# FAVOR attention and a float64 bilinear FFN on one core: whole projections, fillers in early gaps, the clamp on GpSimd, pairs from chunk 6

## The chip, the core and the metric

The kernel runs on one core of a Trainium2 chip. The metric is device microseconds of one execution; lower is better. The times shown are medians over a few runs, and one further execution was taken with the hardware profiler.

The engines are TensorE (PE in the rows; PEld is its weight load), VectorE (DVE), ScalarE (ACT), GpSimd (POOL) and SyncE (SP, which issues most of the DMAs). Each works through its own list of instructions in order.

## The reference: what is computed

Eight sequences of 576 tokens, eight heads of 64 channels, go through an attention with random features; its output, 4608 tokens of 512 channels, goes through a bilinear feed-forward part whose four weights come as float64.

```python
def phi(x):                       # x scaled by 64 ** -0.25
    proj = einsum('bhsd,md->bhsm', x, omega)          # 128 features
    h = proj - sum(x * x, -1, keepdims=True) / 2
    return exp(h - max(h, -1, keepdims=True)) / sqrt(m)
q_p, k_p = phi(q_s), phi(k_s)
kv  = einsum('bhsm,bhsd->bhmd', k_p, v)
num = einsum('bhsm,bhmd->bhsd', q_p, kv)
den = einsum('bhsm,bhm->bhs', q_p, sum(k_p, 2))[..., None] + 1e-06
x = (num / den) -> [4608, 512]
a = x @ w1                        # float64 weights, 512 x 1024
b = x @ w2
out = ((a * b) @ w3) @ w_out      # 1024 x 1024, 1024 x 512
```

The kernel folds `w3 @ w_out` into one matrix `W` of 1024 x 512 on the chip.

## The kernel before

**Tiling.** Tokens go in 36 chunks of 128. For a chunk of k or of q, `features` (line 681) projects eight heads onto 128 features. Operands have 64 rows (one head), so two matmuls, one on the upper and one on the lower 64 rows of the array, stand side by side. Chunks that come early (`whole`) are projected in fp32, 8 matmuls; the later ones (55 projections) are split into two fp16 halves and take three passes, 24 matmuls `pa<-om,hl`. Then VectorE reduces (`s_nm<-pa`) and subtracts, ScalarE takes the exponential, and the result is split into fp16 halves `ek` or `eq`. `kv_batch` sums k features times v, `q_attend` (826) multiplies q features with that, `x_turn` splits and transposes the result into `xT`.

**The feed-forward part.** For chunks below `SG` = 8, `gate` (1127) multiplies `xT` with both weights; from chunk 4 on it takes two chunks at a time, 192 matmuls of 256 columns for two chunks. From chunk `SG` on, `pair_turn` (877) and `pair_gate` (1244) work on two chunks with seven products where eight are usual: 2 x 7 x 24 = 336 matmuls of 128 columns for two chunks, with weight sums that `mix` (1171) makes beforehand on GpSimd. `project_out` (1284) multiplies with `W`: 24 matmuls of 512 columns for a chunk.

**The float64 weights.** `from_float64` (966) turns a piece of 128 x 1024 doubles into fp32: DMA, absolute value on ScalarE, then on VectorE a clamp (`TENSOR_SCALAR arena<-arena` f32), a shift and mask (the same name, uint32) and two combinations (`SCALAR_TENSOR_TENSOR` into `arena`, then into `w12b`). There are 20 such pieces, one of them cut in two; three raw buffers hold them. `W_block` (1065) multiplies w3 with w_out in fp32, 8 products of 8 matmuls `pm<-w12b`.

**What sets the order.** All operations are first recorded, in an order given by a table of slots; consecutive matmuls into the same PSUM tile are joined to one operation of at most `JOIN` = 8 parts (record, line 219). Then a planner (`order`, 411) gives every operation a cost (`cost`, 279), runs a list schedule forwards (`forward`, 322), once backwards for ranks, forwards again, and emits every engine's instructions in the order of the planned starts. Operations cannot be interleaved within: an operation of 8 matmuls is the unit that may alternate with other work. PSUM has two tags: `pa`, two tiles of two banks for projections, kv and attention, and `pm`, four banks for everything else. Nearly all rows carry line 168, the helper that fires a recorded operation, so rows are told apart by their tiles.

Of the kernel before, what the change touches and what calls it, by code (L numbers as in the profile page):

```python
# [8 lines left out]
F32 = mybir.dt.float32  # L9
# [5 lines left out]
ALU = mybir.AluOpType  # L15
# [40 lines left out]
SPARE = 'oh'  # L56
KQ = 's'
TAIL = 2
SG = 8
MIX_N = 3  # L60
MIX_E = 'p'
SUM_E = 'p'
# [139 lines left out]
    return name, p, p + ap.partition_size(), lo * w, hi * w  # L202


def flat(a):
    return a.ap if isinstance(a, View) else a


class Plan:
# [9 lines left out]
    def record(self, lane, method, args, kwargs):  # L219
# [59 lines left out]
    def cost(self, op):  # L279

        out = op.out
        n = out.free_size()
        m = max([n] + [a.free_size() for a in op.ins])
        if op.lane == "tensor":
            t = 0
            for p in op.parts:
                c = p.out.free_size() / 2.4 + 2.5
                if p.ins[0].dtype == F32:
                    c = 4 * p.out.free_size() / 2.4 + 5
                if p.ins[0].partition_size() == 64:  # L290
                    c = c / 2 + 2
                t += max(c, 27)
            return t, t + 170
        if op.method == "dma_start":
            size = n * out.partition_size() * mybir.dt.size(out.dtype)
            return {"sync": 330, "scalar": 100, "gpsimd": 680}[op.lane], size / 330
        if op.method == "dma_start_transpose":
            return 2140, 1300
        thin = [a for a in op.ins if a.free_size() == 1 and m > 1]
        if op.lane == "vector":  # L300
            wide = [a for a in op.ins if a.free_size() > 1]
            if op.method == "memset":
                t = 10 + 0.8 * n * mybir.dt.size(out.dtype) / 4
            elif op.method == "reciprocal":
                t = 85 + 4 * n
            elif op.method == "tensor_reduce" or len(wide) > 1:
                t = 72 + 1.1 * m + (60 if thin else 0)
            else:
                t = 68 + 0.53 * m + 45 * len(thin)
            return t, t + 85  # L310
        if op.lane == "scalar":
            t = (130 if thin else 60) + 0.9 * m + (60 if "accum_out" in op.kwargs else 0)
            return t, t + 95
        if op.method == "memset":
            t = 40 + 0.85 * n
        elif op.method == "tensor_tensor":
            t = 95 + 2.0 * m
        else:
            t = 100 + 1.0 * m
        return t, t + 50  # L320

    def forward(self, rank, deps, after, costs, slots=False):
# [4 lines left out]
        dma = 0.0  # L327
        free, todo, slot, line = {}, {}, {}, {}
        if slots:
            for g in self.gens:  # L330
# [23 lines left out]
        for _ in self.ops:  # L354
# [15 lines left out]
            busy, lat = costs[op]  # L370
# [40 lines left out]
    def order(self):  # L411
# [12 lines left out]
        best = None  # L424
        self.seen = []
        plain = {o: set(o.deps) for o in ops}
        for n in range(ROUNDS):
            start, total, slot = self.forward(rank, plain, turned(plain), costs, True)
            self.seen.append(total)
            deps = self.chained(start, slot)  # L430
            after = turned(deps)
            for m in range(INNER + 1):
                if m:
                    start, total, _ = self.forward(rank, deps, after, costs)
# [4 lines left out]
                late, _, _ = self.forward(  # L439
                    back, {o: set(after[o]) for o in ops}, {o: list(deps[o]) for o in ops}, costs  # L440
                )
                rank = {o: -late[o] - costs[o][0] for o in ops}
        _, start, slot = best
        for g, k in slot.items():
            g.slot = k
        return sorted(ops, key=lambda o: (start[o], o.index))

    def emit(self):
        before = {}
# [3 lines left out]

ROOM = {"xhl1": 1024}
BANKS = ("pm", "pa")
JOIN = 8
HOP = 60
ROUNDS = 1
INNER = 2
AHEAD = 500  # L460
# [3 lines left out]
def tile_favor_attention_then_bilinear_ffn(  # L464
# [41 lines left out]
    ps = Slots(nc, ps)  # L506

    def banks(name):
        return ps.tile([P, 2, 512], F32, tag="pa", name=name, bufs=2)
# [6 lines left out]

    ones_bf = const.tile([P, P], BF16, name="ones_bf")
    nc.vector.memset(ones_bf, 1.0)
    ln_e = const.tile([P, 1], F32, name="ln_e")
    nc.vector.memset(ln_e, 15 * math.log(2.0))  # L520

# [6 lines left out]
    def pick(kinds, i):  # L528
        return kinds[min(i, len(kinds) - 1)]
# [426 lines left out]
    left = {}  # L956
    converted = []
    nfetch = [-1]

    def used(at):  # L960

# [4 lines left out]
    def from_float64(new, src, name, cuts=1):  # L966
# [551 lines left out]
```

## Time and profile before

| | before |
|---|---|
| median of 3 runs | 839.0 us (838.31 to 839.31) |
| the profiled execution | 838.5 us, of which span 836.7 us |
| PE busy | 773.0 us, 92% |
| DVE busy | 627.6 us, 75% |
| ACT busy | 476.2 us, 57% |
| POOL busy | 376.5 us, 45% |

Shares over the whole span hide that the program has stages: float64 conversion and the first chunks (to about 200 us), attention and gates together (to about 700 us), then gates and output alone. A busy PE is not PE at its peak: the matmuls are pipelined, so "mean ns of one" is a latency, and the pace is read from the starts of consecutive rows in the timeline.

### The profile page before, as it was taken

The page shows a single profiled execution, that of the slowest core. Times are in us where ns is not written, and L with a number is a line of the kernel's source. Part 1 is how long each engine was busy: PE and PEld are TensorE (multiplying, and loading weights), DVE is VectorE, ACT ScalarE, POOL GpSimd, SP SyncE. Part 2 cuts the span into 40 slices and gives each one's busy share as a digit, 9 for nine tenths or more (in the row PEclk, how much of TensorE's full clock was granted, in tenths as well). Part 3 has the DMA queues.
Part 4 walks back from the last instruction along what each step waited for, and adds up shares of the span by engine and source line. Part 5 has one row for each costly group of instructions (what it writes and reads, how often), then busy time and mean ns, then how long its engine had stood idle before and what let it go on. Part 6 is the DMA issues. An engine that isn't in the chain of part 4 may idle for free.

```text
span 836.7 us, 24077 instructions
## 1 busy us (share of the span) xinstructions
PE 773.0 (92%) x10376; PEld 587.1 (70%) x10376; DVE 627.6 (75%) x1079; ACT 476.2 (57%) x832; POOL 376.5 (45%) x340
## 2 busy tenths in 40 slices
PE   4697897998989999999899989999999999999998
PEld 4364356876757767777677777778778777888785
DVE  6788989997897787899899978998996761421210
ACT  5776378776657555768577666776743332232221
POOL 0000000649898525475456554765672552331221
PEclk9998799999999999999999999999999999999999
DMA  9695666142543444566538636665435334123001
GB/s 334 216 282 177 195 194 164 27 88 67 120 90 84 84 116 106 103 115 159 109 82 149 153 89 113 128 129 113 87 83 103 69 67 76 40 52 59 19 21 38
DMA packets 164138, 94.16 MB, mean 113 GB/s; under 512 B 138240, under 2 KB 138624, under 8 KB 164032
## 3 DMA queue, kind: packets, MB, share of 16 engines
q1 hardware_dynamic: 163520, 91.58, 46.1%
q8 instruction: 81, 1.33, 0.7%
q10 hardware_dynamic: 432, 0.79, 0.3%
q0 software_dynamic: 80, 0.26, 0.1%
q14 instruction: 25, 0.20, 0.1%
HBM read 49.35 MB, written 9.44 MB: 70 GB/s over the span
## 4 chain that ended last, share of the span: by engine, by line
PE 56%; DVE 27%; issue 6%; ACT 5%; DMA 3%; POOL 2%; SPq 0%; DVEq 0%; ACTq 0%; POOLq 0%
PE pm L168 46%; PE pa L168 10%; DVE s_nm L168 4%; DVE hl L168 3%; DVE e L168 3%; DVE xhl L168 2%; DVE asb L168 2%; DVE arena L168 2%; DVE w12b L168 2%; DVE eq L168 2%; DMA arena<-w 2%; POOL asb L168 1%; ACT e L168 1%; DVE vhl L168 1%; DVE Wb L168 1%
## 5 line engine op out<-in xcount | busy, mean ns | idle before, releaser
L168 PE MATMUL pm<-xT,w12b 128*128 128x128 f16 (+1 forms) x3504 | 285.4, 226 | 11.2 <-DVE asb L168 4.3
L168 PEld LDWEIGHTS <-w12b 128*128 128x128 f16 x3744 | 248.1, 99 | 53.7 <-issue 9.7
L168 PEld LDWEIGHTS <-arena 128*128 128x128 f16 x2832 | 196.0, 98 | 72.9 <-issue 4.0
L168 PE MATMUL pm<-xT,arena 128*128 128x128 f16 x2184 | 186.6, 220 | 2.9 <-DVE asb L168 2.4
L168 PE MATMUL pm<-Wb,arena 128*128 128x512 f16 (+1 forms) x648 | 147.1, 371 | 0.6 <-DVE Wb L168 0.4
L168 POOL TENSOR_TENSOR arena<-asb,arena 128x512 f16<-128x512 f32 x65 | 82.9, 1282 | 116.3 <-ACT arena L168 116.1
L168 DVE TENSOR_REDUCE s_nm<-pa 128x8 f32<-128x1024 f32 x72 | 87.5, 1215 | 23.2 <-PE pa L168 22.9
L168 POOL TENSOR_TENSOR eq<-e,eq 128x1024 f16<-128x1024 f32 x31 | 73.6, 2373 | 66.8 <-DVE eq L168 34.7
L168 POOL TENSOR_TENSOR asb<-asb,asb 128x512 f32<-128x512 f32 x36 | 51.2, 1422 | 107.9 <-DVE asb L168 93.8
L168 ACT ACTIVATE e<-e,ln_e,s_es 128x1024 f32<-128x1024 f32 x55 | 68.1, 1238 | 41.7 <-DVE e L168 41.5
L168 ACT CAST arena<-asb 128x512 f16<-128x512 f32 x65 | 39.5, 614 | 87.6 <-POOL asb L168 56.3
L168 DVE SCALAR_TENSOR_TENSOR asb<-pm,asb 128x512 f32<-128x512 f32 x56 | 38.2, 684 | 61.3 <-PE pm L168 61.2
L168 PE MATMUL pm<-w12b 128*128 128x512 f32 x128 | 64.0, 655 | 13.2 <-DVE w12b L168 13.2
L168 PE MATMUL pa<-om,hl 64*128 64x128 f16 x1320 | 65.8, 220 | 11.1 <-DVE e L168 5.1
L168 POOL TENSOR_TENSOR ek<-e,ek 128x1024 f16<-128x1024 f32 x26 | 58.5, 2249 | 34.3 <-ACT ek L168 29.9
L168 DVE TENSOR_TENSOR e<-pa,s_nm 128x1024 f32<-128x1024 f32 x59 | 71.6, 1213 | 0.8
L168 DVE SCALAR_TENSOR_TENSOR xhl<-xs,s_p2r,xhl 128x768 f16<-128x768 f32 (+2 forms) x36 | 47.0, 1312 | 29.0 <-ACT xhl L168 29.0
L168 DVE TENSOR_TENSOR asb<-pm,asb 128x512 f32<-128x512 f32 x72 | 48.0, 682 | 26.8 <-PE pm L168 26.3
L168 PEld LDWEIGHTS <-hl 64*128 64x128 f16 x1320 | 38.1, 94 | 35.0 <-issue 16.8
L168 POOL TENSOR_TENSOR xs<-xs 128x256 f32<-128x256 f32 x56 | 44.3, 806 | 30.2 <-DVE xs L168 28.9
L168 PE MATMUL pm<-Wb,w12b 128*128 128x512 f16 x240 | 57.3, 382 | 0.0
L168 PEld LDWEIGHTS pm<-w12b 128*128 128x128 f32 x128 | 26.0, 210 | 44.3 <-issue 33.5
(114 smaller groups left out, 1160.9 us busy)
## 6 DMA issues: line engine op xcount, KB each, us to landing
vraw<-v SPq DMA_DIRECT2D x36, 256.0 KB, 3.0
qraw<-qT SPq DMA_DIRECT2D x35, 256.0 KB, 2.9
out<-o SPq DMA_DIRECT2D x34, 256.0 KB, 2.5
arena<-w3T SPq DMA_DIRECT2D x8, 1024.0 KB, 5.5
kraw<-kT SPq DMA_DIRECT2D x32, 256.0 KB, 3.0
arena<-w SPq DMA_DIRECT2D x8, 1024.0 KB, 6.5
arena<-wo SPq DMA_DIRECT2D x3, 1024.0 KB, 5.6
eqT<-eq SPq DMA_TRANSPOSE x72, 3.3
```

The source lines that it names most:

```text
L168: p.real = getattr(lanes[p.lane], p.method)(*args, **{k: real(a) for k, a in p.kwargs.items()})
```

## The change

- **Projections whole.** `rows(op)` is the number of rows or columns that the stationary operand uses. Matmuls into one tile are joined only with others of the same `rows`, up to 24 parts; those of under 128 rows without limit. So a projection is one operation.
- **The planner knows changes of rows.** `forward` adds 105 ns where TensorE goes from one `rows` to another, and in the forward passes after the first it ranks an operation with other `rows` 1000 ns later. Costs of DMA issues, of small matmuls and the hop between engines (`HOP` 60 to 80) change as well. A class `Gate` can model the clock; as set (`WARM = True`) it leaves every matmul at full speed.
- **Fillers.** After planning, `fill` looks for planned gaps of TensorE before 200 us and puts matmuls of ones, 128 x 512, into an idle `pm` bank; nobody reads them.
- **The clamp** of the first piece stays on VectorE, the other 20 instructions go to GpSimd.
- **Pairs from chunk 6:** `SG` 8 to 6, so chunks 6 and 7 go through `pair_turn` and `pair_gate`.

```diff
+CLAMP = "dp"
-SG = 8
+SG = 6
+def rows(op):
+    return min(op.ins[0].partition_size(), op.ins[0].free_size())
...
             and prior.lane == "tensor"
-            and len(prior.parts) < JOIN
+            and (len(prior.parts) < JOIN or rows(op) < 128)
+            and rows(op) == rows(prior)
...
-            return {"sync": 330, "scalar": 100, "gpsimd": 680}[op.lane], size / 330
+            return {"sync": 480, "scalar": 300, "gpsimd": 700}[op.lane], size / 330
...
-            op = min(can, key=lambda o: rank[o])
+            if n == "tensor" and tiling:
+                op = min(can, key=lambda o: rank[o] + (rows(o) != tiling) * TURN * scale)
+            else:
+                op = min(can, key=lambda o: rank[o])
...
+            if n == "tensor":
+                if tiling and tiling != rows(op):
+                    busy += 105
+                tiling = rows(op)
...
+    def fill(self, start, costs):
...
+        for o in line:
+            a, b = end, start[o]
+            end = b + costs[o][0]
+            n = int((b - a - GAP) // 216)
+            if n <= 0 or a > UNTIL:
+                continue
...
+            stuff.parts = [
+                Op("tensor", "matmul", (out, self.ones, self.ones[:, 0:1].broadcast_to([128, 512])),
+                   {"start": True, "stop": True})
+                for _ in range(n)
+            ]
+            stuff.index = o.index
+            start[stuff] = a + 1
...
-JOIN = 8
-HOP = 60
+JOIN = 24
+FIRST, GAP, UNTIL = 1500.0, 300.0, 200000.0
+TURN = 1000.0
+WARM = True
+HOP = 80
...
-                nc.vector.tensor_scalar(g, g, F64_TOP, F64_LEAST, ALU.min, ALU.max)
+                (nc.gpsimd if pick(CLAMP, nfetched.pop(0)) == "p" else nc.vector).tensor_scalar(
+                    g, g, F64_TOP, F64_LEAST, ALU.min, ALU.max
+                )
```

Where it moves instructions, three places. On TensorE, at the first fp16 projection of the program (`hl` is the split input, `om` the features' matrix, `Wb` and `arena` the operands of the output product), before:

```order
L168 MATMUL pa_84<-om,hl_1705 128x128
L168 LDWEIGHTS arena
L168 MATMUL pm_298<-Wb,arena 128x512
...
L168 LDWEIGHTS hl_1705
L168 MATMUL pa_84<-om,hl_1705 128x128
...
L168 LDWEIGHTS w12b
L168 MATMUL pm_330<-xT_1092,w12b 128x128
```

And after:

```order
L169 LDWEIGHTS w12b
L169 MATMUL pm_81<-xT_1211,w12b 128x128
L169 LDWEIGHTS hl_1887
L169 MATMUL pa_84<-om,hl_1887 128x128
...
L169 LDWEIGHTS w12b
L169 MATMUL pm_117<-xT_1211,w12b 128x128
```

Before, eight matmuls of the projection alternate with eight of other work; now its 24 stand in one block. Counted over TensorE's whole list, the matmuls go from 64 rows to 128 or back 345 times before and 114 times after; from this first fp16 projection on it is 318 and 90.

At TensorE's start (`kraw` is the raw k chunk, `o` the buffer that lends its place to chunk 2), before:

```order
L168 MATMUL pa_84<-om_raw,kraw_77 128x128 x8
L168 MATMUL pa_164<-om_raw,kraw_127 128x128 x8
L168 LDWEIGHTS ones_bf
L168 MATMUL pm_81<-om_sq,ones_bf 128x1
L168 MATMUL pa_84<-om_raw,o_78 128x128 x8
```

And after:

```order
L169 LDWEIGHTS ones_bf
L169 MATMUL pm_81<-ones_bf 128x512
L169 MATMUL pa_84<-om_raw,kraw_77 128x128 x8
L169 MATMUL pa_172<-om_raw,kraw_140 128x128 x8
L169 LDWEIGHTS ones_bf
L169 MATMUL pm_81<-om_sq,ones_bf 128x1
L169 LDWEIGHTS ones_bf
L169 MATMUL pm_116<-ones_bf 128x512
...
L169 MATMUL pa_84<-om_raw,o_78 128x128 x8
```

Nine fillers now stand ahead of the first projection and 23 behind the norm of omega; with seven later groups it is 127.

At GpSimd's start (`vhl` are cleared margins of v, `arena` the float64 pieces), before:

```order
L168 MEMSET vhl_136 64x520
L168 DMA qraw_214<-qT 128x512
L168 MEMSET vhl_96 128x8 x2
...
L168 ISA
L168 TENSOR_TENSOR arena<-asb_88,arena 128x512
```

And after:

```order
L169 MEMSET vhl_137 64x520
L169 ISA
L169 TENSOR_SCALAR arena<-arena 128x512
L169 TENSOR_SCALAR arena<-arena 128x1024
L169 DMA qraw_271<-qT 128x512
L169 TENSOR_SCALAR arena<-arena 128x1024 x9
...
L169 TENSOR_SCALAR arena<-arena 128x1024 x7
L169 TENSOR_TENSOR arena<-asb_88,arena 128x512
L169 TENSOR_SCALAR arena<-arena 128x1024 x2
```

GpSimd's list now begins with the 20 clamps; the q load and part of the clearing of v stand behind some of them.

## Rows read from the trace of the kernel before

**Rows 1.** The page: the span, and busy time of the engines.

```profile
span 836.7 us, 24077 instructions
PE 773.0 (92%) x10376; PEld 587.1 (70%) x10376; DVE 627.6 (75%) x1079; ACT 476.2 (57%) x832; POOL 376.5 (45%) x340
```

**Rows 2.** Busy time by stretch: stretch, length, each engine's us, PEclk, DMA.

```profile
0.00:200.00 200.00, 163.96 (x1498) 113.84 (x1499) 173.45 (x299) 134.32 (x281) 41.94 (x56) 0.95 0.60 180
300.00:650.00 350.00, 333.98 (x5386) 260.33 (x5384) 313.74 (x539) 226.14 (x366) 197.09 (x170) 0.99 0.54 113
```

**Rows 3.** Whom PE waited for, 200 to 700 us: total, times, longest.

```profile
PE pm L168 <- DVE asb L168: 6.9, 5, 3.5
...
PE pa L168 <- DVE xs L168: 2.4, 4, 0.9
```

**Rows 4.** Whom DVE waited for longest, 200 to 700 us.

```profile
DVE s_gd L168 <- PE pa L168: 20.4, 10, 5.6
```

**Rows 5.** Timeline of PE near 217 us: start, us, operation, count.

```profile
216.16 0.61 PE L168 MATMUL pm<-xT,w12b 128*128 128x128 f16 x8
216.71 1.07 PE L168 MATMUL pa<-om,hl 64*128 64x128 f16 x32
217.71 1.05 PE L168 MATMUL pm<-xT,w12b 128*128 128x256 f16 x8
218.69 0.40 PE L168 MATMUL pa<-om,hl 64*128 64x128 f16 x8
219.01 0.39 PE L168 MATMUL pm<-xT,w12b 128*128 128x256 f16 x2
```

**Rows 6.** Timeline of PE near 746 us, without projections.

```profile
745.20 1.89 PE L168 MATMUL pm<-Wb,arena 128*128 128x512 f16 x8
746.92 0.61 PE L168 MATMUL pm<-xT,arena 128*128 128x128 f16 x8
747.37 1.89 PE L168 MATMUL pm<-Wb,arena 128*128 128x512 f16 x8
```

**Rows 7.** Fp16 projections by stretch: PE's busy time on tile hl.

```profile
300.00:650.00 350.00, 49.69 (x992) 0.99 0.54 113
```

**Rows 8.** Groups of DVE by shape: busy us, mean ns of one.

```profile
L168 DVE SCALAR_TENSOR_TENSOR asb<-pm,asb 128x512 f32<-128x512 f32 x56 | 38.2, 684 | 61.3 <-PE pm L168 61.2
L168 DVE SCALAR_TENSOR_TENSOR hl<-kraw,s_s,hl 128x512 f16<-128x512 f32 x25 | 38.1, 1522 | 0.0
L168 DVE SCALAR_TENSOR_TENSOR arena<-arena 128x1024 uint32<-128x1024 uint32 x19 | 23.1, 1217 | 0.1
L168 DVE TENSOR_SCALAR arena<-arena 128x1024 uint32<-128x1024 uint32 x19 | 13.4, 707 | 0.0
L168 DVE TENSOR_SCALAR arena<-arena 128x1024 f32<-128x1024 f32 x19 | 13.0, 686 | 3.6 <-ACT arena L168 3.4
```

**Rows 9.** Groups of POOL by shape.

```profile
L168 POOL TENSOR_TENSOR eq<-e,eq 128x1024 f16<-128x1024 f32 x31 | 73.6, 2373 | 66.8 <-DVE eq L168 34.7 <-ACT e L168 10.9 <-DVE s_gd L168 9.4
L168 POOL MEMSET vhl<- 64x520 f32 x2 | 1.1, 525 | 0.1
```

**Rows 10.** Timeline of PE, fp32 products of w3 and w_out, idle before.

```profile
39.97 8.80 PE L168 MATMUL pm<-w12b 128*128 128x512 f32 x16 [3.29 <-DVE w12b L168]
48.61 0.59 PE L168 MATMUL pm<-asb,ones_bf 128*128 128x512 bf16 x2
87.44 9.40 PE L168 MATMUL pm<-w12b 128*128 128x512 f32 x16 [6.43 <-DVE w12b L168]
96.78 1.16 PE L168 MATMUL pa<-om_raw,qraw 64*128 64x128 f32 x16
97.87 3.70 PE L168 MATMUL pm<-w12b 128*128 128x512 f32 x8
101.50 0.72 PE L168 MATMUL pa<-om_raw,kraw 64*128 64x128 f32 x8
```

**Rows 11.** PE by stretch: busy us, granted clock, DMA share.

```profile
78.40:92.00 13.60, 6.03 (x30) 0.50 0.74 236
```

More of the change, by code (lines that the diff above doesn't have):

```diff
@@ L202, in box, with __init__, run, turn @@
     return name, p, p + ap.partition_size(), lo * w, hi * w
+def rows(op):
+    return min(op.ins[0].partition_size(), op.ins[0].free_size())
 def flat(a):
     return a.ap if isinstance(a, View) else a
+class Gate:
+    def __init__(self):
+        self.warm, self.end, self.work, self.at = WARM, WINDOW, 0.0, 0.0
+    def run(self, t, busy, work):
+        total = 0.0
+        while t >= self.end:
+            self.turn()
+        while True:
+            k = 1.0 if self.warm else 2.0
+            room = self.end - t
+            if busy * k <= room:
+                self.work += work * k
+                return total + busy * k
+            done = room / (busy * k)
+            self.work += work * k * done
+            total += room
+            t = self.end
+            busy, work = busy * (1 - done), work * (1 - done)
+            self.turn()
+    def turn(self):
+        share = self.work / WINDOW
+        if WARM is not True:
+            self.warm = share > 0.4 if self.warm else share > 0.75
+        self.end += WINDOW
+        self.work = 0.0
 class Plan:
@@ L320, in cost, with forward @@
         return t, t + 50
-    def forward(self, rank, deps, after, costs, slots=False):
+    def forward(self, rank, deps, after, costs, slots=False, backwards=False, scale=0.0):
         start, end, waiting, ready = {}, {}, {}, {n: [] for n in LANES}
@@ L327, in forward @@
         dma = 0.0
+        tiling, gate = None, Gate()
         free, todo, slot, line = {}, {}, {}, {}
@@ L366, in forward @@
             t, n, can = best
-            op = min(can, key=lambda o: rank[o])
+            if n == "tensor" and tiling:
+                op = min(can, key=lambda o: rank[o] + (rows(o) != tiling) * TURN * scale)
+            else:
+                op = min(can, key=lambda o: rank[o])
             ready[n].remove(op)
             start[op] = t
-            busy, lat = costs[op]
+            busy, lat = costs[op][:2]
+            if n == "tensor":
+                if tiling and tiling != rows(op):
+                    busy += 105
+                tiling = rows(op)
+                if not backwards:
+                    busy = gate.run(t, busy, costs[op][2])
+                lat += busy
             clock[n] = t + busy
@@ L426, in order @@
         plain = {o: set(o.deps) for o in ops}
+        scale = TURN0
         for n in range(ROUNDS):
-            start, total, slot = self.forward(rank, plain, turned(plain), costs, True)
+            start, total, slot = self.forward(rank, plain, turned(plain), costs, True, scale=scale)
             self.seen.append(total)
@@ L433, in order @@
                 if m:
-                    start, total, _ = self.forward(rank, deps, after, costs)
+                    start, total, _ = self.forward(rank, deps, after, costs, scale=1.0)
                     self.seen.append(total)
@@ L439, in order @@
                 late, _, _ = self.forward(
-                    back, {o: set(after[o]) for o in ops}, {o: list(deps[o]) for o in ops}, costs
+                    back,
+                    {o: set(after[o]) for o in ops},
+                    {o: list(deps[o]) for o in ops},
+                    costs,
+                    backwards=True,
                 )
                 rank = {o: -late[o] - costs[o][0] for o in ops}
+                scale = 1.0
         _, start, slot = best
@@ L445, in order @@
             g.slot = k
-        return sorted(ops, key=lambda o: (start[o], o.index))
+        start = dict(start)
+        self.fill(start, costs)
+        return sorted(start, key=lambda o: (start[o], o.index))
+    def fill(self, start, costs):
+        busy = {}
+        for g in self.gens:
+            if g.ops and g.tag == "pm":
+                a = min(start[o] for o in g.ops)
+                b = max(start[o] + costs[o][0] for o in g.ops) + 2 * HOP + 170
+                busy.setdefault(g.slot, []).append((a, b))
+        line = sorted((o for o in self.ops if o.lane == "tensor"), key=lambda o: start[o])
+        end = FIRST
+        for o in line:
[4 more added lines that the diff above has]
+                continue
+            idle = [
+                (max([y for x, y in t if y <= a + HOP] + [0]), k)
+                for k, t in busy.items()
+                if not any(x < b and y > a for x, y in t)
+            ]
+            if not idle:
+                continue
+            gen = Gen(self.bank_pool, "pm", [128, 512], F32, 4)
+            gen.slot = min(idle)[1]
+            out = View(gen, gen.pool.base(gen, gen.slot))
+            stuff = Op("tensor", "matmul", (), {})
+            stuff.parts = [
+                Op("tensor", "matmul", (out, self.ones, self.ones[:, 0:1].broadcast_to([128, 512])),
+                   {"start": True, "stop": True})
+                for _ in range(n)
+            ]
+            stuff.index = o.index
+            start[stuff] = a + 1
     def emit(self):
@@ L455 @@
 BANKS = ("pm", "pa")
-JOIN = 8
-HOP = 60
+JOIN = 24
+FIRST, GAP, UNTIL = 1500.0, 300.0, 200000.0
+TURN = 1000.0
+TURN0 = 0.0
+WINDOW = 3413.0
+WARM = True
+HOP = 80
 ROUNDS = 1
@@ L518, in tile_favor_attention_then_bilinear_ffn @@
     nc.vector.memset(ones_bf, 1.0)
+    nc.ones = ones_bf
     ln_e = const.tile([P, 1], F32, name="ln_e")
@@ L958, in tile_favor_attention_then_bilinear_ffn @@
     nfetch = [-1]
+    nfetched = list(range(99))
     def used(at):
```

18 lines of the change are left out of this document (9 added, 9 removed).

## The prediction

> **What bounds the kernel now.** I read the busy times first [rows 1]: TensorE works 773 of 836.7 us, VectorE 628. Shares over the whole span mix stages, so next the stretches [rows 2]. To 200 us TensorE has 164 of 200 us and VectorE 173: the float64 conversion and the first features keep VectorE full, and TensorE's 36 idle us are waits for it and for loads. From 300 to 650 us TensorE has 334 of 350 and VectorE 314: TensorE is the bound, with VectorE close behind. The waits say the same: from 200 to 700 us TensorE waits 23.5 us in all (five rows, 6.9 down to 2.4) [rows 3], while VectorE's longest entry alone, a wait for TensorE, makes 20.4 us [rows 4]. So a microsecond of TensorE's own work behind 200 us is mostly a microsecond of the end, as long as VectorE can follow; before 200 us what counts is how early VectorE is done.
>
> The trace's own time is 838.5 us (span 836.7 and 1.8 around it); the median of the runs, 839.0, is 0.5 above. I sum against the trace and add the 0.5 at the end.
>
> **Projections whole.** The price of a change of rows is in the timeline [rows 5, 6]. A block of 32 projection matmuls takes 217.71 - 216.71 = 1.00 us to the next start, one of 8 takes 219.01 - 218.69 = 0.32. The 24 between them cost 0.68, or 0.028 each; 8 x 0.028 = 0.23, so leaving a block costs 0.09. Entering: 8 gate matmuls of 128 columns ahead of the block take 216.71 - 216.16 = 0.55 [rows 5], ahead of other 128-row work 747.37 - 746.92 = 0.45 [rows 6], so 0.10. I take 0.096 for either. The order counts 345 changes before and 114 after: 231 x 0.096 = 22.2 us of TensorE, nearly all behind 190 us, since 228 of the 231 fall behind the first fp16 projection. The projections lie where TensorE is the bound: 992 of their 1320 matmuls between 300 and 650 us [rows 7].
>
> Is all of it on the path? VectorE has 36 idle us in those 350 [rows 2], and 0.75 x 22.2 = 17 us would be taken out of them; it can follow, with 19 us left. But blocks get coarser: an output product of 24 matmuls now holds TensorE for 24 x 0.215 = 5.2 us where its blocks of 8 held it for 746.92 - 745.20 = 1.72 [rows 6], while a VectorE that waits for `pa` cannot be served. I take nine tenths, **-20**, bounds -5 (below, first rival) and -22.
>
> **Pairs from chunk 6.** Chunks 6 and 7 take 192 matmuls of 256 columns before, at (0.98 - 0.10) / 8 = 0.110 us [rows 5] 21.1 us; after, 336 of 128 columns at 0.45 / 8 = 0.056 [rows 6], 18.8 us. **-2.3.** What comes with it, four combinations of 0.68 us on VectorE [rows 8], wider splits, six more GpSimd additions, lies beside TensorE's work; without that cover VectorE's four alone are 2.7 us. Mixed weights are due one pair earlier; chunks 4 and 5 and output products still stand ahead.
>
> **The clamp.** VectorE loses 19 x 0.686 + one half piece of about 0.42 [rows 8]: 13.5 us of its 173. GpSimd gains 20 instructions of a kind that the trace doesn't show. Bounds: clearing 520 elements takes 0.525 us [rows 9], so 1024 at least 1.03; a two-input operation of 1024 takes 2.37 [rows 9]. With one input I take 1.2, near the lower row.
>
> These are not free for VectorE. `SCALAR_TENSOR_TENSOR` of 512 with one input in PSUM takes 684 ns; with both in SBUF (`hl`), 1522 on average, in a stretch in which GpSimd is busy half of the time [rows 2, 8]. The operations that remain in a converted piece (shift 0.707, two combinations of 1.2) [rows 8] are of such kinds, so a clamp on GpSimd can hold them up for its length. How often? These three alone make 19 x 3.1 = 59 of VectorE's 160 us that are left before 200, or 0.37; with the splits that also read two SBUF inputs I take 0.55, an estimate. At 1.2 us, 20 x 1.2 x 0.55 = 13 us come back. **0**, bounds -13.5 and +34 (20 x 2.37 - 13.5).
>
> [...]
>
> **Fillers.** 127 matmuls of 512 columns at 0.215 [rows 6] are 27.3 us, meant for TensorE's 36 idle us before 200 [rows 2]. Part will not fit: where data come sooner than planned, real work stands behind fillers in TensorE's order, and VectorE's reduction behind that. Bounds 0 and +27 (all in the way); I take **+1.5**, since a late projection there costs only what VectorE, busy with conversions, doesn't cover. [...] **-3**, bounds 0 and -6.
>
> **The planner's new costs** (hop, DMA issue) reorder all engines. Nothing in the trace prices that; 0, with 4 us to either side.
>
> Sum: 838.5 - 20 - 2.3 + 0 + 1.5 - 3 = 814.7 on the trace, and with the 0.5 **815 us** as median.
>
> **Rivals.**
> 1. *VectorE holds the pace from 300 to 650 us.* The saved TensorE time there becomes waiting: blocks of 5.2 us delay the two `pa` tiles, and each 1.2 us reduction then starts later. For: VectorE is busy 314 of 350 [rows 2]. Against: its waits there are waits for TensorE [rows 4]. Then only a quarter of the changes of rows pays, 5.5 us: 838.5 - 5.5 - 2.3 + 1.5 - 3 + 0.5 = **830 us**.
> 2. *GpSimd's clamps block VectorE (slower).* Each takes as long as a two-input operation, 2.37 us, and blocks in full: +34 on VectorE before 200 us, where it is the bound, so 815 + 34 = **849 us**. It decides above +24, that is from (24 + 13.5) / 20 = 1.9 us lost for each clamp. Against: one input, not two, and VectorE also runs reductions that read PSUM (asb's 684 ns are undisturbed [rows 8]). [...]
> 3. *Everything pays.* All of the 22.2, the 6 of the clock, and half of the 13.5, since blocked operations are few: 838.5 - 22.2 - 2.3 - 6 - 6.7 + 0.5 = **802 us**.
> 4. *The change doesn't do what it says*: the plan's blocks are already in the order that I counted, so this can hold for the fillers alone, if the clock falls all the same: +3 to the forecast, within its range.
>
> **Numbers.** Forecast (808 to 823 us) 0.60, everything pays 0.14, VectorE's pace 0.17, blocked by clamps 0.09. The range that leaves out no more than 2 in 10 takes the third rival's time as its lower end and the first's, with a microsecond, as its upper: 801 to 831. A measurement of this kernel can tell about 0.2%, 1.7 us, from no change. Faster by more than that: the forecast, the third rival and 0.13 of the first, 0.87. Within it: the other 0.04 of the first, where waits of the new plan cost VectorE more than in its time above. Slower: the second, 0.09.
>
> **What would show it.** Right: 8 gate matmuls ahead of a projection and the block's end still cost 0.09 to 0.10 each, but the blocks stand in 24s and 48s; TensorE's busy time from 300 to 650 us stays near 95% while more chunks leave per us; its waits from 200 to 700 us stay near 23 us; the last attention's `s_gd` comes earlier by about as much as the end. [...] The granted clock before 200 us shows whether fillers hold it. Wrong: TensorE idle well above 5% from 300 to 650 us with VectorE as releaser (first rival), or VectorE busier than 173 us in the first 200 (second rival).

## The result and the profile after

The changed kernel takes **814.9 us** (median of four runs, 811.4 to 815.6) where 815 was forecast. Beside it the kernel before ran at 838.7 us; the ratio is 0.971, with a 95% interval of 0.968 to 0.974, so 24 us are gone. The profiled execution took 815.6 us.

The page of the kernel after, its span and busy times, to be held against [rows 1]:

```profile
span 813.5 us, 24647 instructions
PE 769.2 (95%) x10647; PEld 597.7 (73%) x10647; DVE 619.2 (76%) x1061; ACT 475.5 (58%) x834; POOL 407.3 (50%) x366
```

TensorE's busy time hardly falls, since 127 fillers count in it. The stretches of [rows 2], after (stretch, length, busy us of PE, PEld, DVE, ACT and POOL, granted clock, DMA):

```profile
0.00:200.00 200.00, 190.92 (x1794) 128.47 (x1796) 177.54 (x297) 145.98 (x298) 79.77 (x86) 0.99 0.65 186
...
300.00:650.00 350.00, 325.81 (x5453) 268.32 (x5452) 310.05 (x542) 221.60 (x362) 200.78 (x174) 0.98 0.53 112
```

To 200 us the granted clock went from 0.95 to 0.99 (for before that share is too high, as e1 shows). From 300 to 650 us TensorE is busy *less* than before (326 against 334 of 350), and so is VectorE, while only 67 matmuls more leave. TensorE's waits there grew; the view of [rows 3] after, 200 to 700 us, adds up to 31.5 us where before had 23.5:

```profile
PE pm L169 <- ACT asb L169: 10.5, 10, 3.0
PE pa L169 <- DVE xs L169: 9.0, 6, 3.8
PE pa L169 <- DVE e L169: 8.0, 7, 5.1
PE pm L169 <- DVE asb L169: 2.9, 5, 1.3
```

Two events cut the span into an early part, a middle and a tail: the first transfer of a result on SyncE's queue (`out<-o`; the first chunk's result leaves by ScalarE's queue, in before and after some 10 us earlier) and the last division of an attention (`s_gd<-pa`). In these rows of after the second of the two numbers behind the durations, "to", is the last start, the first one the first start:

```profile
L169 SPq DMA_DIRECT2D out<-o x5: 359/385/529, 186.1 to 287.8; - x5
L169 DVE TENSOR_SCALAR s_gd<-pa x12: 148/157/167, 504.4 to 668.2; 128x8 f32<-128x8 f32 x12
```

Read in the same way from each trace (us; the middle is the difference of the two columns before it):

| kernel | first result on SyncE's queue | last `s_gd` | middle | span |
|---|---|---|---|---|
| before | 198.7 | 694.5 | 495.8 | 836.7 |
| after | 186.1 | 668.2 | 482.1 | 813.5 |
| without fillers (e1) | 194.6 | 676.2 | 481.6 | 821.0 |
| projections cut again (e3) | 187.0 | 680.8 | 493.8 | 825.8 |
| before with the new joins alone (e4) | 198.6 | 667.2 | 468.6 | 810.6 |
| after with the old planner (e6) | 187.7 | 661.3 | 473.6 | 806.1 |
| after without knowledge of rows (e8) | 184.3 | 662.5 | 478.2 | 807.5 |
| e6 with 128-row blocks of 8 (e11) | 194.7 | 678.4 | 483.7 | 817.5 |

So after gains 12.6 us early, where 1.5 had been forecast, and 13.7 in the middle, where 22 had been; 3 go back in the tail. Where early ends is a matter of the marker: by the sixth division of an attention (192.3 us before, 175.7 after) 16.6 us are early and 9.7 in the middle. By either, the total was met by two errors of opposite sign, and the experiments say where each lies.

### The profile page after: what moved, and what is told of

Read it like the earlier page. It is cut to its first block, busy times and chain, and to the rows that moved or that the text cites. A ratio compares the mean times of both kernels' runs of the same rounds, so it can differ in the third digit from the quotient of the medians.

```text
span 813.5 us, 24647 instructions
## 1 busy us (share of the span) xinstructions
PE 769.2 (95%) x10647; PEld 597.7 (73%) x10647; DVE 619.2 (76%) x1061; ACT 475.5 (58%) x834; POOL 407.3 (50%) x366
## 4 chain that ended last, share of the span: by engine, by line
PE 41%; DVE 26%; ACT 9%; POOL 9%; issue 7%; DMA 6%; SPq 0%; DVEq 0%; ACTq 0%; POOLq 0%
PE pm L169 36%; PE pa L169 5%; DVE s_nm L169 4%; DVE vhl L169 3%; DVE w12b L169 3%; DVE hl L169 3%; DVE e L169 3%; ACT e L169 3%; POOL asb L169 2%; DVE xhl L169 2%; POOL xs L169 2%; POOL arena L169 2%; DMA xT<-xhl 2%; DVE asb L169 2%; DVE arena L169 2%
## 5 line engine op out<-in xcount | busy, mean ns | idle before, releaser
L169 PEld LDWEIGHTS <-w12b 128*128 128x128 f16 x3720 | 238.6, 99 | 51.5 <-issue 14.6
L169 PEld LDWEIGHTS <-arena 128*128 128x128 f16 x2988 | 203.7, 98 | 76.0 <-issue 9.9
L169 PE MATMUL pm<-xT,w12b 128*128 128x128 f16 (+1 forms) x3480 | 247.1, 225 | 8.2 <-ACT asb L169 8.0
L169 PE MATMUL pm<-xT,arena 128*128 128x128 f16 x2340 | 171.2, 220 | 4.8 <-ACT asb L169 4.4
L169 PE MATMUL pm<-Wb,arena 128*128 128x512 f16 (+1 forms) x648 | 141.3, 376 | 1.2 <-DVE asb L169 1.2
L169 DVE TENSOR_TENSOR e<-pa,s_nm 128x1024 f32<-128x1024 f32 x59 | 71.2, 1211 | 0.3
L169 POOL TENSOR_SCALAR arena<-arena 128x1024 f32<-128x1024 f32 (+1 forms) x20 | 23.3, 1165 | 95.6 <-ACT arena L169 93.1
L169 POOL TENSOR_TENSOR xs<-xs 128x256 f32<-128x256 f32 x60 | 51.0, 867 | 31.1 <-DVE xs L169 30.3
L169 DVE TENSOR_TENSOR asb<-pm,asb 128x512 f32<-128x512 f32 x72 | 48.9, 682 | 13.9 <-PE pm L169 12.8
L169 PE MATMUL pm<-w12b 128*128 128x512 f32 x128 | 56.8, 596 | 0.3 <-DVE w12b L169 0.3
L169 ACT ACTIVATE xhl<-xs,s_p2r 128x768 f16<-128x768 f32 (+2 forms) x36 | 35.2, 984 | 31.6 <-DMA xT<-xhl 17.7
L169 PE MATMUL pa<-om,hl 64*128 64x128 f16 x1320 | 45.9, 218 | 7.4 <-DVE xs L169 6.4
```

Of the source, the lines that this page charges most:

```text
L169: p.real = getattr(lanes[p.lane], p.method)(*args, **{k: real(a) for k, a in p.kwargs.items()})
```

## The experiments

Two theories at first. **A**: the forecast's terms hold, changes of rows are worth about 0.09 us each on the path. **B**: the early part (fillers, clamp) brings the gain and the middle is held by VectorE. The runs were measured in three lots, each with its own runs of before (839.0, 838.8 and 838.2 us), so differences between lots are good to about half a microsecond. A difference of two kernels has an interval of some 3 us to either side; what lies within it is called so.

**e1: after without the fillers**, the rest of the order as it was.

```diff
-        self.fill(start, costs)
```

> The changed kernel without its 127 fillers; the order of every engine is otherwise the same. Theory A, the prediction's own sum: fillers bring 3 and cost 1.5 us, so 816 to 817. Theory B, from the two traces (at the sixth attend the changed kernel is 12 us ahead, so most of the gain of the first 200 us has to come from clamp and fillers): fillers are worth 5 us or more, so 820 or above, with the granted clock before 200 us falling as it did before the change.

Measured: 822.7 us, ratio 0.981 (0.979 to 0.982). The fillers are worth **7.8 us**, as B had it. TensorE's busy time and the granted clock in the first 30 us, and to 200 us, of e1:

```profile
0.00:30.00 30.00, 15.27 (x88) 11.30 (x89) 19.44 (x38) 18.53 (x54) 6.81 (x15) 0.72 0.93 330
...
0.00:200.00 200.00, 170.13 (x1581) 122.82 (x1582) 171.36 (x286) 138.32 (x286) 71.61 (x81) 0.90 0.64 182
```

The same of after, the first 30 us:

```profile
0.00:30.00 30.00, 27.42 (x161) 14.15 (x162) 19.91 (x39) 19.13 (x57) 5.84 (x15) 1.00 0.93 335
```

Without fillers the granted clock falls to half again and again (0.50 from 12 to 22 us, for one; means of 0.72 in the first 30 us and 0.90 to 200 us); with them it stands at 1.00 and 0.99. For before the view gives 1.00 up to 30 us, but its rows don't bear that out. The same sixteen products in before, in e1 and in after:

```profile
15.62 2.08 PE L168 MATMUL pa<-om_raw,hl 64*128 64x128 f32 x16 [1.12 <-ACT ek L168]
14.30 2.08 PE L169 MATMUL pa<-om_raw,hl 64*128 64x128 f32 x16 [0.91 <-ACT ek L169]
14.68 1.16 PE L169 MATMUL pa<-om_raw,hl 64*128 64x128 f32 x16 [1.39 <-ACT ek L169]
```

They take as long in before as in e1 (2.08 us), where the clock is at 0.50, so before was slow there as well, and fillers win in a place where its clock row showed no loss. VectorE gets its products sooner: the last conversion of a weight (`w12b<-arena`) starts at 142.1 us in e1 and at 133.7 after, 8.4 us that are found again at the first result (8.5), at the last `s_gd` (8.0) and at the end. Here e1:

```profile
L169 DVE SCALAR_TENSOR_TENSOR w12b<-arena x2: 1214/1216/1218, 129.0 to 142.1; 128x1024 uint32<-128x1024 uint32 x2
```

**e2: the clamps back on VectorE**, after planning, so that the order stays.

```diff
         self.fill(start, costs)
+        for o in ops:
+            if o.lane == "gpsimd" and o.method == "tensor_scalar":
+                o.lane = "vector"
```

> The changed kernel with the 20 clamps back on VectorE, each at the place of the plan; nothing else moves. Theory A: clamps on GpSimd give VectorE 13.5 us and take as much back by blocking, so 815, within 2. Theory B: GpSimd's clamps hardly block (in the trace of the changed kernel shift and combinations keep 0.68 and 1.21 us in the median), VectorE is the bound before 200 us, and most of 13 us come back: 822 to 828.

Measured: 817.5 us, 0.975 (0.973 to 0.976): the clamp on GpSimd is worth 2.7 us by the medians, at the edge of what can be told; the profiled executions differ by 0.2. Neither 822 to 828 nor nothing. The three kinds of operation of a converted piece that stay on VectorE, after (count, busy us, mean ns):

```profile
L169 DVE SCALAR_TENSOR_TENSOR w12b<-arena 128x1024 uint32<-128x1024 uint32 x19 | 24.8, 1315 | 0.1
L169 DVE SCALAR_TENSOR_TENSOR arena<-arena 128x1024 uint32<-128x1024 uint32 x19 | 23.9, 1260 | 0.2
...
L169 DVE TENSOR_SCALAR arena<-arena 128x1024 uint32<-128x1024 uint32 x19 | 13.0, 683 | 5.7 <-POOL arena L169 5.7
```

And the clamp itself on GpSimd, after, by its tile (min, median and max ns):

```profile
L169 POOL TENSOR_SCALAR arena<-arena x20: 613/1042/2048, 10.1 to 123.0; 128x1024 f32<-128x1024 f32 x19, 128x512 f32<-128x512 f32 x1
```

Against 707, 1217 and 1267 ns before, these three kinds are only 19 x (1315 - 1267 + 1260 - 1217 + 683 - 707) = 1.3 us longer. But before has another order and its means hold other collisions. e2 has after's order, so VectorE's operations can be held against each other one by one: up to the last conversion of a weight (`w12b<-arena`), nine that overlap a clamp are longer in after, by 6.0 us together. Two of them, each with the clamp beside it on POOL, after:

```profile
39.58 2.10 DVE L169 SCALAR_TENSOR_TENSOR arena<-arena 128x1024 uint32<-128x1024 uint32 x1
39.56 1.04 POOL L169 TENSOR_SCALAR arena<-arena 128x1024 f32<-128x1024 f32 x1 [0.74 <-ACT arena L169]
...
81.13 1.00 DVE L169 TENSOR_SCALAR s_nm<-s_nm 128x8 f32<-128x8 f32 x1
80.06 2.05 POOL L169 TENSOR_SCALAR arena<-arena 128x1024 f32<-128x1024 f32 x1 [3.59 <-ACT arena L169]
```

And the same two operations in e2:

```profile
40.16 1.22 DVE L169 SCALAR_TENSOR_TENSOR arena<-arena 128x1024 uint32<-128x1024 uint32 x1
...
81.85 0.16 DVE L169 TENSOR_SCALAR s_nm<-s_nm 128x8 f32<-128x8 f32 x1
```

So the blocking is 6.0 us, not 13 and not 1.3, and 2.5 of it fall on three operations of 128 x 8 that take 0.16 us by themselves. Reductions that read `pa` overlap whole clamps and are no longer for it (1214 ns at 13.6 us, 1211 in e2). The clamp can be the one that is held up: beside VectorE's `eq<-e,eq` (1.21 us from 80.00 us on) it takes 2.05 us instead of 1.04 (at 80.06 us, above).

VectorE's time up to the last conversion tells the rest. The 20 clamps take 13.6 us of VectorE in e2; without them its busy time falls only from 124.4 to 118.6 us, and its idle time grows from 11.6 to 15.2, 5.7 of it waits for GpSimd. That leaves 2 us, and the last conversion starts 2.3 us earlier, at 133.7 instead of 136.0. Moving the clamps took little off VectorE; what it did take off came through. This is e2's row:

```profile
L169 DVE SCALAR_TENSOR_TENSOR w12b<-arena x1: 1215/1215/1215, 136.0 to 136.0; 128x1024 uint32<-128x1024 uint32 x1
```

**e3: projections cut again, in place.** In after's finished order a projection of 24 matmuls and the 24 matmuls of 128 rows ahead of it alternate in eights where no dependency forbids it: 274 changes of rows instead of 114. The other engines' lists stay; but the first operation of a pair now ends later, by two pieces of the projection (0.7 us), and so does whatever waits for it, which counts into the price below.

```diff
+            new[a] = [pieces[0]]
+            new[b] = [pieces[3], pieces[1], pieces[4], pieces[2], pieces[5]]
```

> The changed kernel's plan, but where a block of 24 matmuls with 128 rows stands ahead of a projection of 24, the two alternate in eights as before the change: 274 changes of rows in place of 114, the same matmuls, the other engines' orders untouched. Theory A (a change costs 0.096 us and nine tenths of it are on the path): 160 x 0.096 x 0.9 = +14, so 829. Theory B (the middle is held by VectorE and by handoffs as well): about half, +7, so 822. If the change of rows cost nothing: 815.

Measured: 827.7 us, 0.986 (0.985 to 0.988), 12.8 us more than after for 160 changes: **0.080 us each**, 83% of 0.096 (the interval reaches from about 0.06 to 0.10). The last `s_gd` moves by 12.6. TensorE's busy time grows by 15.7 us, 0.098 for each change, and its waits from 200 to 700 us fall by 4.4 (31.5 to 27.1). The page of e3, to be held against after's:

```profile
PE 784.9 (95%) x10647; PEld 596.3 (72%) x10647; DVE 619.9 (75%) x1061; ACT 476.6 (58%) x834; POOL 405.2 (49%) x366
```

TensorE's timeline in e3 shows the price itself (start, us, operation, count):

```profile
308.46 0.62 PE L169 MATMUL pm<-xT,arena 128*128 128x128 f16 x8
309.02 0.40 PE L169 MATMUL pa<-om,hl 64*128 64x128 f16 x8
309.35 0.62 PE L169 MATMUL pm<-xT,arena 128*128 128x128 f16 x8
```

Eight gate matmuls take 309.02 - 308.46 = 0.56 to the next start, as in [rows 5], eight of a projection 0.33. This is A, and against VectorE holding all of the middle.

**e4: before, with the new joins alone.** The old planner with its old costs, clamps on VectorE, no fillers, `SG` 8; 125 changes of rows.

```diff
+def rows(op):
+    return min(op.ins[0].partition_size(), op.ins[0].free_size())
...
-            and len(prior.parts) < JOIN
+            and (len(prior.parts) < JOIN or rows(op) < 128)
+            and rows(op) == rows(prior)
...
-JOIN = 8
+JOIN = 24
```

> The kernel before with nothing but the longer joins (operations of one tiling, 24 parts, projections without limit), planned anew by the old planner with its old costs: 125 changes of rows in place of 345. Theory A: 220 x 0.096 x 0.9 = 19 us less than before, 820. Theory B: half of it, about 829; the rest of the gain would be from the other parts. If coarse blocks starve VectorE: 839 or above.

Measured: 812.0 us, 0.968 (0.967 to 0.970): **27 us from the joins alone**, no worse than the whole change, and more than either theory allowed. The first result on SyncE's queue leaves when it did before (198.6 us), and the sixth division of an attention comes 5.7 us earlier (186.6); most of the gain lies behind. From 300 to 650 us, e4:

```profile
300.00:650.00 350.00, 332.08 (x5607) 270.47 (x5605) 321.23 (x567) 229.28 (x375) 207.12 (x181) 1.00 0.55 117
```

TensorE is as busy as before, issues 221 matmuls more than before in the same time, and VectorE follows with 321 us instead of 314. The granted clock is 1.00. So the middle can give all of the forecast and more; in after something takes about half of it back. That is the question of the second lot: **C**, the planner's new costs, or **P**, the wider work of the pairs.

**e5, e6, e7: pairs and planner apart.** e5 is after with `SG` back at 8. e6 is after with the old planner: old costs, `HOP` 60, no price and no rank for changes of rows. e7 is both. All are planned anew.

```diff
-SG = 6
+SG = 8
```

> The changed kernel with SG = 8 again, planned anew: chunks 6 and 7 through the plain gate. The joins alone gave 812.0, fillers are worth 7.8 and the clamp 2.6 in place, so something in the change takes some 13 us back behind 200 us. Theory P: the pairs do, since mixed weights are due earlier while GpSimd is full from 180 to 260 us; then 803 to 808. Theory C: the planner's new costs do; then pairs only save their 2.3 us and this gives 817.

```diff
-                op = min(can, key=lambda o: rank[o] + (rows(o) != tiling) * TURN * scale)
+            op = min(can, key=lambda o: rank[o])
...
-                if tiling and tiling != rows(op):
-                    busy += 105
...
-            return {"sync": 480, "scalar": 300, "gpsimd": 700}[op.lane], size / 330
+            return {"sync": 330, "scalar": 100, "gpsimd": 680}[op.lane], size / 330
...
-HOP = 80
+HOP = 60
```

> The changed kernel with the planner's old costs (no price and no rank for a change of rows, hop 60, old DMA and matmul costs); joins, fillers, clamp and pairs stay. Theory C (the new costs take 13 us back): 799 to 803. Theory P (the pairs do): 813 to 816.

> As the run before, and SG = 8 too: longer joins, fillers and the clamp on GpSimd alone. If parts add: 812.0 - 7.8 - 2.6 = 801.6 by either theory. If the early lead is given back whatever plan stands behind it (VectorE holds the middle): 811.

Measured: e5 813.6 us (0.969, 0.967 to 0.972), e6 **806.9** (0.962, 0.960 to 0.964), e7 806.4 (0.962, 0.959 to 0.965). Pairs from chunk 6 are worth nothing that can be told, with either planner (+1.3 and +0.5 us by the medians). The new planner costs 7.9 us with pairs from 6, 7.2 with pairs from 8. e6 and e7 are faster than both kernels of this case. None of the expected ranges was met: e5 lies between P and C, nearer C, e6 between them too, and e7 between 801.6 and 811, so the parts don't simply add: fillers and clamp are worth 10.5 us when taken out of after (e1, e2), and 5.6 on top of the joins. In a ladder of medians: before 838.7, joins 812.0 (-27), with fillers and clamp 806.4 (-5.6), with the new planner 813.6 (+7.2), with pairs from 6, which is after, 814.9 (+1.3).

**e8: after without the knowledge of rows alone** (the price of 105 ns and the rank of 1000 ns), with its other new costs; 122 changes of rows.

> The changed kernel whose planner neither prices a change of rows (105 ns) nor ranks by it (1000 ns); hop, DMA and matmul costs stay new; 122 changes of rows in place of 114. Theory C in the narrow form (knowing changes of rows makes it choose worse orders): 800 to 805. If hop and DMA costs are what matters: 812 to 816. If knowing them is worth what it saves: 8 x 0.096 = 0.8 us more, 816.

Measured: 809.3 us, 0.966 (0.963 to 0.969): of the planner's 7.9 us, 5.6 (some 2 to 9 by the intervals) are the knowledge of rows (800 to 805 was expected by one theory, 812 to 816 by the other; 809.3 lies between). It saves eight changes and costs more than they are worth. A place where it may, from TensorE's timeline of after (in brackets the idle time ahead and its releaser):

```profile
361.97 0.84 PE L169 MATMUL pa<-om,hl 64*128 64x128 f16 x24
363.63 0.85 PE L169 MATMUL pa<-om,hl 64*128 64x128 f16 x24 [0.81 <-DVE xs L169]
...
367.13 1.50 PE L169 MATMUL pm<-xT,w12b 128*128 128x128 f16 x24
373.72 1.48 PE L169 MATMUL pa<-kv,eqT 128*128 128x65 f16 x24 [5.09 <-DVE e L169]
```

And VectorE in the same place:

```profile
363.50 1.04 DVE L169 SCALAR_TENSOR_TENSOR vhl<-vraw,s_s,vhl 128x512 f16<-128x512 f32 x1
...
369.06 1.14 DVE L169 SCALAR_TENSOR_TENSOR vhl<-vraw,s_s,vhl 64x512 f16<-64x512 f32 x1
370.13 1.21 DVE L169 TENSOR_REDUCE s_nm<-pa 128x8 f32<-128x1024 f32 x1
371.33 1.20 DVE L169 TENSOR_REDUCE s_nm<-pa 128x8 f32<-128x1024 f32 x1
372.46 1.20 DVE L169 TENSOR_TENSOR e<-pa,s_nm 128x1024 f32<-128x1024 f32 x1
373.73 1.19 DVE L169 TENSOR_TENSOR e<-pa,s_nm 128x1024 f32<-128x1024 f32 x1
```

Two projections stand one behind the other, which spares a change of rows. They fill both `pa` tiles at once. VectorE comes to them only at 370.13, behind five splits of v (`vhl<-vraw`) that its own order puts first; then it makes four passes of 1.2 us, and the attention, which needs a `pa` tile, waits 5.09 us, until the first tile's subtraction is done. Such double blocks of 48 occur ten times in after, nine in e8, five in e6, six in e4, so the count doesn't separate e8; nor do TensorE's waits in all (34.1 us in e8, 31.5 after). The longest wait for `e` does (2.3 us in e8, 5.1 after). That the knowledge of rows costs 5.6 us is shown; that it does so by this wait is not. Behind the wait the granted clock is 0.55 (374 to 380 us), as the next experiment shows.

**e12: after, with TensorE kept busy in two waits.** Ahead of the attention at 374 us and of a projection that waits 3.8 us at 582 us, the first matmul of the operation in front is issued 60 and 50 times more; it writes what it writes anyway.

```diff
+            o.parts = [o.parts[0]] * more + o.parts
```

> The changed kernel with repeated matmuls in front of two of its longest waits (60 ahead of the attend that waits 5.1 us at 374 us, 50 ahead of the projection that waits 3.8 us at 582 us); each repeats the first matmul of the operation before, so it writes what is written anyway. If the half clock behind these waits (6.8 us each in the trace) costs what it looks like, 2 x 3.4: 808 to 809. If the waits themselves are the loss and the clock is beside the path: 815, and up to 6 more where the repeats delay who waits for that operation.

Measured: 812.0 us, 0.969 (0.967 to 0.971), 2.8 less than after, within what two intervals allow, and between the two expectations. The trace is plainer. From 374 to 380 us, after:

```profile
374.00:380.00 6.00, 6.00 (x54) 4.55 (x52) 5.88 (x10) 5.97 (x7) 2.13 (x1) 0.55 0.25 46
```

And e12:

```profile
374.00:380.00 6.00, 5.03 (x62) 3.44 (x62) 6.00 (x12) 5.46 (x8) 2.13 (x1) 1.00 0.23 44
```

TensorE at 0.55 is busy without a break and gets less done than at 1.00 with a sixth of the time idle. All stretches at half clock from 200 to 700 us together, read from the windows: before 6.8 us, after 24, e4 3.4, e6 13.6, e8 6.8, e12 6.8. If half of each were lost, after would lose 8.6 us more than before, and its waits are 8.0 longer [rows 3]: 16.6 us, more than the 8.5 that its middle lacks against the forecast. By the same account e8 would be better by 8.6 of clock less 2.6 of longer waits, 6.0 (measured 5.6), and e6 by 5.2 and 3.8 (waits of 27.7), 9.0 (measured 7.9). But e12, the one run that was made to test the clock, doesn't fit: 8.5 of clock and 1.5 of waits (30.0 in all) would make 10 us, and 2.8 were measured. One reason is in the rows. From 208.8 to 215.4 us after runs at 0.50 and e12 at 1.00, though nothing was changed there; yet the attention behind starts no sooner, first after, then e12:

```profile
220.80 0.90 PE L169 MATMUL pa<-kv,eqT 128*128 128x65 f16 x24 [2.24 <-DVE xs L169]
221.14 1.48 PE L169 MATMUL pa<-kv,eqT 128*128 128x65 f16 x24 [5.08 <-DVE xs L169]
```

Here the slow stretch stood ahead of a wait for VectorE and cost nothing. Of the two stretches that e12 took away on purpose, each worth 3.4 us if half is lost, the first gave 1.0 us from the block at 363.63 to the one at 396.68, the second 2.7 from the block at 573.47 to the one at 590.01. So the account shows where clock may be lost, not what it costs.

**e9 and e10: which engine holds the middle.** e9 leaves out 4 of the 24 matmuls of the output products in 18 chunks, so that those outputs lack a part of the sum: 15.6 us less for TensorE. e10 takes the largest magnitude of a row in 27 chunks from 64 of 512 columns: 27 x (0.676 - 0.209) = 12.6 us less for VectorE.

```diff
+            o.parts = o.parts[:8] + o.parts[12:]
```

> The changed kernel without 4 of the 24 matmuls in the output products of 18 chunks (the sixth to the 23rd, some 300 to 650 us); a twelfth part of the sum over the hidden width, twice over, is left out of these outputs. 18 x 4 x 0.216 = 15.6 us of TensorE's work are gone, no order changes. If TensorE holds the middle, nine tenths show at the end: 801. If VectorE holds it, most turns into waiting: 809 or above.

```diff
+            o.args = (o.args[0], o.args[1][:, :, 0:32]) + tuple(o.args[2:])
```

> The changed kernel whose row maximum of the attention's output is taken over 64 of 512 columns for 27 chunks (the ninth to the 35th), so that the scale of the split is from an eighth of the row. Each such reduction falls from 0.675 us to about 0.15: 27 x 0.52 = 14 us of VectorE's work are gone, no order changes. If VectorE holds the middle: 803 to 806. If TensorE holds it: 812 to 815.

Measured: e9 811.6 us (0.968, 0.965 to 0.971), e10 811.8 (0.969, 0.966 to 0.972): 3 us less each, at the edge of what can be told, and far from 15.6 and 12.6. In e9 the work that was taken out came back as waits, 300 to 650 us:

```profile
PE pm L169 <- ACT asb L169: 11.0, 10, 2.5
PE pa L169 <- DVE e L169: 9.2, 5, 5.1
PE pa L169 <- DVE xs L169: 8.8, 5, 3.8
```

31.8 us in all, 24.0 after. In e10 the reductions were shortened as meant (group of VectorE):

```profile
L169 DVE TENSOR_REDUCE s_mx<-xs 128x1 f32<-128x64 f32 x27 | 5.5, 209 | 0.2
```

e10 comes out nearly as expected if TensorE holds the middle, e9 as expected if VectorE does. So in after's order neither engine alone holds the middle; that they hold each other, in turns that the order fixes, fits both runs. Each was taken from a finished order; what a new plan would make of it wasn't tried.

**e11: are short blocks better elsewhere?** e6 with matmuls of 128 rows joined to 8 instead of 24, projections still whole, planned anew; 138 changes of rows against 130.

```diff
-JOIN = 24
+JOIN = 8
```

> As the run with the planner's old costs (806.9), but only projections are joined without limit; work of 128 rows is cut into operations of 8 parts as before the change (138 changes of rows against 130). If coarse blocks of other work starve VectorE: 801 to 804. If only the number of changes counts: 806.9 + 8 x 0.096, 807 to 808.

Measured: 821.5 us, 0.980 (0.977 to 0.984): 14.6 us *more* than e6, for eight changes of rows, which explain less than 1. Both expectations failed. So with the old planner long blocks of 128 rows are worth 14.6 us, and part of e4's 27 us is likely theirs and not that of whole projections. Each length was planned once only, so what the length itself does and what another turn of the plan does aren't told apart. Nearly all of it arises in the middle: the table's first result is 7.0 us later than in e6, but the one on ScalarE's queue is 0.6 earlier (179.0 against 179.6) and the sixth division only 1.8 later (181.6), while the last `s_gd` is 17.1 later. Through which work wasn't settled.

## Why the total was right, and which steps were not

1. **What bounds the kernel.** Before 200 us VectorE's end was named as what counts, and what brought it forward reached the end: e1's 8.4 us at the last conversion are 7.8 at the end, and e2's 2.3 are 2.7. That step holds. But an operation taken off VectorE isn't its length taken off VectorE's end: of 13.6 us there 2.3 arrived (e2). "A microsecond of TensorE's own work behind 200 us is mostly a microsecond of the end" holds for changes of rows (83%, e3) and fails for output products (3 of 15.6, e9). A share of busy time of 95% (334 of 350 us) didn't tell the two apart. A change of rows lies ahead of a projection, whose result VectorE's reductions wait for; an output product can fill TensorE while it waits for VectorE. That is an explanation of e3 and e9 together, not shown by a run of its own.
2. **Projections whole, -20.** Price and count were right: 0.080 us by experiment, 0.096 by the timeline, 0.9 of it assumed on the path. 231 x 0.080 = 18.5 us, close to the 20. The joins alone gave 27, because the other part of the same rule, 24 parts for work of 128 rows, was costed at a loss: "blocks get coarser" was the reason for taking only nine tenths. e11 shows that long blocks gain in the old planner's plan. Mis-sized by 7 us.
3. **The planner's new costs, 0 with 4 to either side.** The step that failed most in the middle: +7.9 us (e6), twice the bound, 5.6 of it from the price and the rank that keep equal rows together (e8). Nothing in the trace priced it, as the prediction says, and 0 stood for not known. The forecast counted the blocks of 48 as a saving in changes and didn't ask who waits for the tiles that they hold. [rows 4] had VectorE's wait for `pa` as its longest; the reverse, TensorE's wait until VectorE lets go of a `pa` tile, wasn't priced. By which wait the 7.9 us arise stays open: the one shown is 5.09 us long, and e12, which kept the clock up behind it and a second one, got 2.8 us back.
4. **Fillers, +1.5 and -3.** Measured together, as e1 against after: -7.8, beyond even the bound of -6. No run shows the -3 of the sum, nor the 6 of its bound. What the trace of before shows is two blocks of 16 fp32 products that take 8.64 and 9.34 us to the next start, where one of 8 takes 3.63 [rows 10], the second of them at a granted clock of 0.50 [rows 11]. In e1 the loss starts ahead of both: its mean clock is 0.72 already to 30 us, with the same pace in before by its rows. Whether fillers stood in the way somewhere (+1.5) can't be read from the net; TensorE waits 8.9 us to 200 us after, against 36 of idle time before [rows 2].
5. **The clamp, 0.** Measured -2.7, within the bounds of -13.5 and +34, and near 0 by luck. The blocking was 6.0 us instead of 13: how often an operation meets a clamp (0.55) was an estimate, and nine did. The relief was no 13.5 either, since VectorE's idle time up to the last conversion grew by 3.6 us, with 5.7 of waits for GpSimd's clamps in it; the sum had no term for that. The means of the shift and the combinations alone (0.68, 1.26 and 1.32 us after) would have said that a clamp rarely holds VectorE up: most of the blocking is hidden in means over 19 operations or falls on other kinds. Had each of the 20 clamps stood in VectorE's time for the estimated 1.2 us, that would have made 24 us; 6.0 were measured. The clamp itself, taken as 1.2 us, has a median of 1.04 us and a mean of 1.19.
6. **Pairs, -2.3.** Not seen: +1.3 (e5) and +0.5 (e7 to e6), both within the spread. TensorE's time for these chunks lies in the middle, where e9 shows that less work on TensorE alone gives a fifth or less.
7. **The rivals.** The first, VectorE's pace, came in part: TensorE is idle 6.9% from 300 to 650 us, with VectorE as releaser of two thirds of its waits. But its cause was the new order, not the engine's load: e4 runs VectorE at 321 of 350 us. The second fell with e2: 6.0 us of blocking, not 47. The third's 802 us wasn't reached. Of the signs one was badly chosen: VectorE busier than 173 us to 200 us was to speak for blocking by clamps, yet of the 177.5 only 6.0 are blocking, and e2, without it, has 181.1; after reaches later work sooner.

The sum in short: forecast -20 for joins, -1.5 for fillers and clamp, 0 for the planner, -2.3 for pairs, together -24. Found along the ladder: -27, -5.6, +7.2, +1.3, together -24. The total was right to 0.1 us by luck: 11 us of unseen gain met 11 us of unseen loss.

Left open: by which waits the new planner loses its 7 to 8 us; through which work the long blocks of 128 rows gain 14.6 us (e11), and 6 to 9 of e4's 27 us that 220 changes at 0.080 to 0.096 don't cover, probably the same thing.

## What to carry over

Measure the parts of a change to a planner one by one, on the old planner too: here the joins alone were worth as much as the whole change, and taking the planner's new costs back made it 8 us faster. A rule that saves a cost of one engine (a change of rows) should also be priced by the tiles that the saved order fills at once and by who waits for them. To see what two engines do to each other, move the work inside a finished order and compare the operations one by one; means against another order hid most of the blocking here. Where work is taken off a busy engine, ask who waits for that work, not how busy the engine is.

## What the runs showed of the hardware

- The clock of TensorE decided more than was thought, in both directions: 127 products that nobody reads bring 7.8 us, and two waits of 5.1 and 3.8 us are each followed by a stretch in which the granted clock is about 0.55 for 6 us. Repeating a matmul in the wait keeps it at 1.00 (e12), but gave 2.8 us, not 6.8: a stretch at half clock ahead of a wait (208.8 to 215.4 us) cost nothing.
- The clock's row can miss a slow start: up to 30 us before's reads 1.00, while sixteen products take 2.08 us as at 0.50 in e1, against 1.16 after.
- GpSimd's clamp of 1024 columns takes 1042 ns in the median but 1194 in the mean, up to 2048. Nine VectorE operations beside the 20 clamps are longer by 6.0 us in all, some by most of a clamp (1.22 to 2.10 us; a 128 x 8 operation 0.16 to 1.00), while reductions that read PSUM aren't (1214 against 1211 ns).
- Putting 160 changes of rows into a finished order cost 0.080 us each of the end, little less than the 0.09 to 0.10 between the starts in the timeline: such a change is paid nearly in full even in a stretch where TensorE waits 7% of the time.
